# Reordering loads, one weight split and z's transfers in the first phase of a gated-mix kernel

## The chip, the cores and the metric

The kernel runs on one core of a Trainium2 chip. A core has a matrix engine (TensorE, in the profile PE, with its weight loads as PEld), VectorE (DVE), ScalarE (ACT), GpSimd (POOL) and SyncE (SP). Each takes its instructions from a queue of its own, in order. Transfers (DMA) are issued from one of these queues and run beside them on the core's 16 DMA engines. The metric is the device time of one execution in microseconds (us), the median over runs; all times below are us unless marked otherwise.

## The reference

x is 2048 x 512, all in float32. One gate per row mixes two branches.

```python
x = A_x
g = sigmoid((x * gate_w).sum(-1, keepdims=True))
# branch a: linear attention, 32 heads of 16
q, k, v = split_heads(x @ wqkv)
pq, pk = q @ w_phi[h], k @ w_phi[h]                      # per head
phi_q = concat([softmax(pq), softmax(-pq)])              # per head, over 16
phi_k = concat([softmax(pk), softmax(-pk)])
kv = phi_k^T v            ;  z = phi_k summed over all rows
a = (phi_q kv) / (phi_q z + 1e-6) @ wo
# branch b: 512 -> 1376 -> 512
b = mish(x @ w1 + b1) @ w2
out = g * a + (1 - g) * b
```

## The kernel before

**Precision.** Every matmul operand is split into a high part (rounded to fp32r) and a low part (the rest), and each product is three matmuls: high by high, high by low, low by high. So each weight piece and each piece of x needs an ACT step that makes the high part and a DVE or POOL step that subtracts to get the low part.

**Phases.** Phase A walks over x in eight chunks of 256 rows (index 0 to 7; "chunk four" is index 3) and makes q, k, v, the exponentials of k's features, and the sums kv and z. Phase B walks over four blocks of 512 rows: the two big matmuls of branch b (`up`, `down`), phi_q, and the output. While phase A runs, w1, w2 and wo are loaded piece by piece and split, ready for phase B.

**Order.** The order is written out by hand: a text of short names per chunk (FIRST, SECOND, THIRD, FOURTH, SEVEN for index 4 and 5, NEXT for 6, LAST for 7) and per block. `run` (line 209) walks a text and emits the named step; an apostrophe means the step of the chunk before, a plus the first block of phase B, a hash a step of the weights. Each instruction is pinned in that order on its own engine's queue; steps of different engines meet only through their data, their buffers, and the `behind` calls below. In SEVEN the words `more`, `rest` and `late` are replaced by lists of weight steps that differ between index 4 and 5 (lines 886 to 890).

**The steps that the change and the prediction touch**, with the engine of each:

- `ldx` (SP, line 156): loads x two chunks ahead, 512 KB, into one of two buffers of the tag "tx". The sums that `sa` makes stand in buffers of the same tag. `xh` (ACT) and `xl` (DVE, line 258) split the next chunk's x; `sa` (POOL, line 339) forms four sums and differences of it, which `sh0 sh1` (ACT) and `sl0 sl1` (POOL, line 349) split. Index 2 to 5 use these in a scheme with fewer products (matmul steps `s1` to `s7`).
- `mx mn d0 d1` (DVE): per head maximum and minimum of k's features, and the differences, into a tile E; `E` (ACT): its exponential; `S rS` (DVE): sums and reciprocals; `ml` (DVE, line 297): scales E by them. The number behind is the half of the chunk (0 or 1).
- `kk` (PE): the matmuls into `kvp` for two chunks, from E and v. `v0 v1` and `ve0 ve1` make v (PE, ACT); `qe st` copy q (ACT) and store it (SP).
- `z` : up to index 4 a transfer, issued by POOL, that adds E to a sum in DRAM (line 454). `zld` (SP, line 462) loads one such sum into `zacc`, `za` (POOL, line 465) adds the other by a transfer; from index 5 on `z` is a POOL addition to `zacc` (line 452).
- `Lj Hj Oj`: load (SP, line 169), high part (ACT) and low part (POOL, line 526) of weight piece j. Pieces 0 to 2 are w1a, 3 to 5 w1b, 6 to 8 w2a, 9 to 11 w2b. The loads go into two buffers of the tag "oh" in turn, so a load waits for the `O` of the piece two before it in the order of loading (0 1 2 3 4 5 11 7 8 9 6 10).
- `behind(...)` (line 293): makes a POOL step wait for the last DVE step named in `dve[0]` at that place of the text; `ml`, `xl` and phase B's `d1` set it. `O`, `sl1` and the additions of `z` carry it.
- In NEXT, `ldx`, `ldw0`: x for phase B's first block; `ldw1`: half of wo; `lq0+`: q of the first block. `up` of phase B takes `xbh` and then `xbl` (line 559), which are x's halves for the block.

Of the kernel before, what the change touches and what calls it, by code (L numbers as in the profile page):

```python
# [41 lines left out]
    S0 rS0 ml0 S1 rS1 ml1 q0 qe0 st0 q1 qe1 st1  # L42
"""
SECOND = """
    h0# h1# sa z0' z1' k0 mx0 mn0 d00 d10 k1 E0 L0# L1# xh mx1 mn1 d01 d11 v0 E1 S0 rS0 ve0 sh0 ml0 xl sl0 z0 ldx
    v1 S1 rS1 ml1 ve1 q0 qe0 st0 q1 qe1 st1 t2# sh1
"""
THIRD = """
# [1 line left out]
    S0 s5 qa rS0 s4 st1 mx1 mn1 d01 d11 s3 qe0 st0 ml0 O1# L3# z0  # L50
"""
FOURTH = """
    s1 bc E1' S1' rS1' ml1' ve1' s7 m7 sh1' s2 xh s6 ca xl sl1' sa z1' H2# O2# L4# mx0 mn0 d00 d10 E0 ldx v0 ve0 sh0 sl0 H3#
    s4 s5 qa st1 S0 rS0 mx1 mn1 d01 d11 v1 s3 qe0 st0 ml0 O3# L5# z0
"""
SEVEN = """
    s1 bc E1' S1' rS1' ml1' ve1' s7 m7 sh1' s2 kk xh xl sl1' zld sa z1' more mx0 s6 ca mn0 d00 d10 E0 ldx v0 ve0 sh0 sl0 za rest S0 rS0
    s4 s5 qa st1 mx1 mn1 d01 d11 E1 ml0 late v1 S1 rS1 s3 ve1 qe0 st0 ml1
"""
NEXT = """  # L60
    lq0+ k0 xh xl mx0 mn0 k1 kk d00 d10 ldx H9# E0 O9# ldw0 L10# z0' z1' mx1 mn1 d01 d11 H6# E1 S0 rS0 ml0 O6# ldw1 v0 ve0
    S1 rS1 ml1 v1 ve1 q0 mx0+ mn0+ d00+ d10+ z0 z1 qe0 st0 q1 qe1 st1 H10# O10# E0+ lq1+
"""
LAST = """
    k0 mx0 mn0 d00 d10 k1 E0 XH0 kv' mx1 mn1 d01 d11 E1 v0 S0 rS0 ml0 z0 ve0 ldo XH1 mx1+ mn1+ S1 rS1 ml1 d01+ d11+
# [33 lines left out]
def tile_gated_mix(ctx: ExitStack, tc: tile.TileContext, xT, wv, wkT, wqT, bd, w1a, w1b, b1, w2a, w2b, wo, out):  # L99
# [109 lines left out]
    def run(text, key, prev=None, nxt=None):  # L209
        for w in text.split():  # L210
            k = prev if w.endswith("'") else nxt if w.endswith("+") else "W" if w.endswith("#") else key
            for fn in steps.pop((k, w.rstrip("'+#")), ()):
                fn()
# [670 lines left out]
    run(THIRD, ("A", 2), ("A", 1))  # L884
    run(FOURTH, ("A", 3), ("A", 2))
    for c in FAST[2:]:
        w = {4: ("", "H4# O4# L11# H5#", "O5# L7# z0"), 5: ("H11# O11# L8# H7# O7# L9#", "", "H8# O8# L6#")}[c]
        text = SEVEN
        for name, part in zip(("more", "rest", "late"), w):
            text = text.replace(name, part)  # L890
        run(text, ("A", c), ("A", c - 1))
    for c, text in ((NCH - 2, NEXT), (NCH - 1, LAST)):
# [64 lines left out]
```

## Time and profile before

| what | us |
|---|---|
| median of 3 runs | 449.32 (448.28 to 449.78) |
| the profiled execution: its time | 449.89 |
| its span, first to last instruction | 448.2 |
| PE busy in the span | 439.8 |
| DVE, ACT, POOL busy | 322.2, 210.7, 158.7 |
| phase A, until the first `up` that reads `xbl` | 151.6 |

How to read it: a busy PE is a PE with a matmul in its pipeline; the matmuls' ends are modelled. Rows of the timeline give start, duration, engine, line, operation, the tile written, an arrow and the tiles read, the number of instructions merged, and in brackets the idle time before and what ended it. ACT steps all carry the line of the helper that issues them (131), matmuls line 111; they are told apart by their tiles. The chain of waits is followed back from the last instruction. The queue of SP holds only transfers, so a transfer that waits for its buffer holds back those behind it.

### The profile page before, as it was taken

Reading aid. Unit: us, or ns where it says so; the run is one execution under the profiler, and the core shown is the slowest. Engines: PE = TensorE matmul, PEld = TensorE weight load, DVE = VectorE, ACT = ScalarE, POOL = GpSimd, SP = SyncE. Lnnn points to the kernel's source line nnn. Section 1 sums busy time; section 2 is a strip of 40 time slices with the busy share of each in tenths; the row PEclk is TensorE's granted clock in tenths of the full one; section 3 lists DMA queues with packets and bytes.
Section 4 is the critical chain, followed back from the end, with each engine's and each line's share of the span. In section 5 each row is a group of like instructions: output and inputs, shape, how many; then the busy total and the mean of one; then the engine's idle time right before and its main releaser. Section 6 shows DMA issues by size and latency. Waiting matters only on the chain.

```text
span 448.2 us, 7019 instructions
## 1 busy us (share of the span) xinstructions
PE 439.8 (98%) x2748; PEld 358.8 (80%) x2748; DVE 322.2 (72%) x427; ACT 210.7 (47%) x292; POOL 158.7 (35%) x120
## 2 busy tenths in 40 slices
PE   7999999899999999999999999999999999999996
PEld 6888888788888788788787887887887888787885
DVE  2499789988899999899899967486967529701002
ACT  4774644464455656527275343634253544233220
POOL 2297477675467364312022221113212122221211
PEclk8999999999999999999999999999999999999999
DMA  8424827979934200404352141321141302030002
GB/s 283 165 68 170 187 77 169 236 165 255 312 95 130 93 24 8 122 20 125 114 152 75 47 141 48 94 95 47 42 148 48 88 7 94 2 88 7 0 0 94
DMA packets 27320, 46.35 MB, mean 103 GB/s; under 512 B 5908, under 2 KB 14100, under 8 KB 27288
## 3 DMA queue, kind: packets, MB, share of 16 engines
q1 hardware_dynamic: 25528, 39.88, 29.2%
q0 software_dynamic: 1616, 5.77, 6.7%
q8 instruction: 21, 0.34, 0.3%
q10 hardware_dynamic: 144, 0.26, 0.3%
q14 instruction: 11, 0.09, 0.1%
HBM read 23.87 MB, written 13.64 MB: 84 GB/s over the span
## 4 chain that ended last, share of the span: by engine, by line
PE 65%; DVE 6%; issue 1%
PE up L111 27%; PE down L111 26%; PE wo L111 10%; PE num L111 2%; DVE E L297 1%; DVE Sm L281 1%; DVE E L273 1%; DVE mx L266 1%; DVE E L275 1%; DVE xbl L559 1%; DVE Sm L289 1%; DVE io L797 0%; DVE mn L266 0%; PE z L111 0%; PE kvT L616 0%
## 5 line engine op out<-in xcount | busy, mean ns | idle before, releaser
L662 POOL TENSOR_TENSOR l<-act,h 128x512 fp32r<-128x512 f32 x44 | 61.1, 1390 | 219.0 <-ACT h L131 183.0
L131 ACT ACTIVATE act<-up,b1s 128x512 f32<-128x512 f32 x44 | 30.3, 689 | 86.5 <-PE up L111 86.3
L131 ACT ACTIVATE E<-E 128x1024 f32<-128x1024 f32 x32 | 33.7, 1060 | 52.4 <-DVE E L275 38.9
L297 DVE TENSOR_TENSOR E<-E,Sm 128x1024 f32<-128x1024 f32 x32 | 46.4, 1451 | 1.0
L281 DVE TENSOR_REDUCE Sm<-E 128x64 f32<-128x1024 f32 x32 | 38.7, 1210 | 4.3 <-ACT E L131 4.2
L111 PE MATMUL wo<-woh,ohl 128*128 128x512 f32 x128 | 40.7, 389 | 0.0
L111 PE MATMUL down<-w2ah,h 128*128 128x512 f32 x96 | 37.5, 390 | 0.0
L111 PE MATMUL down<-w2ah,l 128*128 128x512 f32 x96 | 37.4, 389 | 0.0
L111 PE MATMUL down<-w2al,h 128*128 128x512 f32 x96 | 37.3, 389 | 0.0
L797 DVE SCALAR_TENSOR_TENSOR io<-down,og_sb,io 128x512 f32<-128x512 f32 x16 | 11.1, 749 | 31.0 <-PE down L111 31.0
L111 PE MATMUL down<-w2bh,h 128*128 128x512 f32 x80 | 31.2, 390 | 0.0
L111 PE MATMUL down<-w2bl,h 128*128 128x512 f32 x80 | 31.1, 389 | 0.0
L111 PE MATMUL down<-w2bh,l 128*128 128x512 f32 x80 | 31.1, 389 | 0.0
L131 ACT ACT_TABLE_LOAD x20 | 25.7, 1283 | 9.8 <-PE up L111 9.5
L771 DVE TENSOR_TENSOR ohl<-num,ohl 128x512 fp32r<-128x512 f32 x16 | 10.2, 678 | 26.4 <-ACT ohl L131 26.4
L131 ACT ACTIVATE h<-act 128x512 fp32r<-128x512 f32 x44 | 27.8, 632 | 1.4
L111 PEld LDWEIGHTS wo<-woh,ohl 128*128 128x128 f32 x128 | 24.0, 188 | 5.1
L111 PE MATMUL up<-xbh,w1ah 128*128 128x512 f32 x96 | 26.2, 394 | 0.0
L111 PE MATMUL up<-xbl,w1ah 128*128 128x512 f32 x96 | 25.8, 390 | 0.3 <-DVE xbl L559 0.3
L111 PE MATMUL up<-xbh,w1al 128*128 128x512 f32 x96 | 25.7, 389 | 0.0
L559 DVE TENSOR_TENSOR xbl<-xraw,xbh 128x1024 fp32r<-128x1024 f32 x8 | 10.1, 1291 | 21.0 <-ACT xbh L131 21.0
L111 PE MATMUL wo<-wol,ohl 128*128 128x512 f32 x64 | 24.9, 389 | 0.0
(155 smaller groups left out, 1012.4 us busy)
## 6 DMA issues: line engine op xcount, KB each, us to landing
xraw<-in_xT_dram SPq DMA_DIRECT2D x16, 512.0 KB, 5.4
eT<-tt SPq DMA_DIRECT2D x128, 64.0 KB, 2.0
zd<-E POOLq DMA_DIRECT2D x10, 512.0 KB, 6.9
pqd<-qs SPq DMA_DIRECT2D x16, 256.0 KB, 4.5
pq<-pqd SPq DMA_DIRECT2D x16, 256.0 KB, 2.9
out_dram<-io SPq DMA_DIRECT2D x16, 256.0 KB, 2.1
raw<-in_w1a_dram SPq DMA_DIRECT2D x3, 512.0 KB, 4.5
raw<-in_w2a_dram SPq DMA_DIRECT2D x3, 512.0 KB, 5.7
```

Source lines behind the costliest of these rows:

```text
L111: return pin(nc.tensor.matmul(*a, **k))
L131: return pin(A_.activation(out_, in_, fn, **k))
L266: pin(V.tensor_reduce(d[name], hv(src()), axis=AX.X, op=op))
L273: pin(V.tensor_sub(E, hv(src()), d["mx"][:, :, None].to_broadcast([P, H, DH])))
L275: ins = pin(V.tensor_sub(E, d["mn"][:, :, None].to_broadcast([P, H, DH]), hv(src())))
L281: pin(V.tensor_reduce(d["S"], hv(d["E"][:, :]), axis=AX.X, op=ALU.add))
L289: at(key, "rS" + n, lambda: pin(V.reciprocal(d["S"], d["S"])))
L297: dve[0] = pin(eng.tensor_mul(hv(d["E"][:, :]), hv(d["E"][:, :]), d["S"][:, :, None].to_broadcast([P, 2 * H, DH])))
L559: dve[0] = pin(V.tensor_sub(xb[b][1][:, :, sl], kt(raw[h], SC), f32(xb[b][0][:, :, sl])))
L662: pin(G_.tensor_sub(U[i]["l"], U[i]["a"], f32(U[i]["h"])))
L771: pin(V.tensor_sub(ohl[h, gp][:, 512:], num[h, gp], f32(ohl[h, gp][:, :512])))
L797: pin(V.scalar_tensor_tensor(io[t], dn[t], og_sb[:, i : i + 1], io[t], op0=ALU.mult, op1=ALU.add))
```

## The change

Six places of the order texts change; no step is added or taken out.

- SECOND: `L0 L1` go to the head of the text and `ldx` directly behind `sa`.
- FOURTH (index 3): `z1'` goes ahead of `sl1' sa`; `ldx` goes ahead of `H2 O2 L4`; `O3 L5` leave this chunk.
- SEVEN: a new word `early` stands behind `z1'`, which itself moves ahead of `sl1'`. For index 4 it is `O3 L5 sl1'`; for index 5 it is `sl1' ldx`, so the load of chunk index 7 goes ahead of `zld`, `L8` and `L9`. (The `ldx` that stays further on in the text finds its step already emitted at index 5.)
- Index 5's last list: `O8 L6` leave it.
- NEXT: `O8 L6` stand behind `xl`; `z1'` goes behind `ml0`; `O6 ldw1` go behind `ml1`.

```diff
 SECOND = """
-    h0# h1# sa z0' z1' k0 mx0 mn0 d00 d10 k1 E0 L0# L1# xh mx1 mn1 d01 d11 v0 E1 S0 rS0 ve0 sh0 ml0 xl sl0 z0 ldx
+    L0# L1# h0# h1# sa ldx z0' z1' k0 mx0 mn0 d00 d10 k1 E0 xh mx1 mn1 d01 d11 v0 E1 S0 rS0 ve0 sh0 ml0 xl sl0 z0
     v1 S1 rS1 ml1 ve1 q0 qe0 st0 q1 qe1 st1 t2# sh1
 """
 FOURTH = """
-    s1 bc E1' S1' rS1' ml1' ve1' s7 m7 sh1' s2 xh s6 ca xl sl1' sa z1' H2# O2# L4# mx0 mn0 d00 d10 E0 ldx v0 ve0 sh0 sl0 H3#
-    s4 s5 qa st1 S0 rS0 mx1 mn1 d01 d11 v1 s3 qe0 st0 ml0 O3# L5# z0
+    s1 bc E1' S1' rS1' ml1' ve1' s7 m7 sh1' s2 xh s6 ca xl z1' sl1' sa ldx H2# O2# L4# mx0 mn0 d00 d10 E0 v0 ve0 sh0 sl0 H3#
+    s4 s5 qa st1 S0 rS0 mx1 mn1 d01 d11 v1 s3 qe0 st0 ml0 z0
 """
 SEVEN = """
-    s1 bc E1' S1' rS1' ml1' ve1' s7 m7 sh1' s2 kk xh xl sl1' zld sa z1' more mx0 s6 ca mn0 d00 d10 E0 ldx v0 ve0 sh0 sl0 za rest S0 rS0
+    s1 bc E1' S1' rS1' ml1' ve1' s7 m7 sh1' s2 kk xh xl z1' early zld sa more mx0 s6 ca mn0 d00 d10 E0 ldx v0 ve0 sh0 sl0 za rest S0 rS0
     s4 s5 qa st1 mx1 mn1 d01 d11 E1 ml0 late v1 S1 rS1 s3 ve1 qe0 st0 ml1
 """
 NEXT = """
-    lq0+ k0 xh xl mx0 mn0 k1 kk d00 d10 ldx H9# E0 O9# ldw0 L10# z0' z1' mx1 mn1 d01 d11 H6# E1 S0 rS0 ml0 O6# ldw1 v0 ve0
-    S1 rS1 ml1 v1 ve1 q0 mx0+ mn0+ d00+ d10+ z0 z1 qe0 st0 q1 qe1 st1 H10# O10# E0+ lq1+
+    lq0+ k0 xh xl O8# L6# mx0 mn0 k1 kk d00 d10 ldx H9# E0 O9# ldw0 L10# z0' mx1 mn1 d01 d11 H6# E1 S0 rS0 ml0 z1' v0 ve0
+    S1 rS1 ml1 O6# ldw1 v1 ve1 q0 mx0+ mn0+ d00+ d10+ z0 z1 qe0 st0 q1 qe1 st1 H10# O10# E0+ lq1+
 """
@@
-        w = {4: ("", "H4# O4# L11# H5#", "O5# L7# z0"), 5: ("H11# O11# L8# H7# O7# L9#", "", "H8# O8# L6#")}[c]
+        w = {
+            4: ("O3# L5# sl1'", "", "H4# O4# L11# H5#", "O5# L7# z0"),
+            5: ("sl1' ldx", "H11# O11# L8# H7# O7# L9#", "", "H8#"),
+        }[c]
         text = SEVEN
-        for name, part in zip(("more", "rest", "late"), w):
+        for name, part in zip(("early", "more", "rest", "late"), w):
             text = text.replace(name, part)
         run(text, ("A", c), ("A", c - 1))
```

More of the change, by code (lines that the diff above doesn't have):

```diff
@@ L44 @@
 SECOND = """
-    h0# h1# sa z0' z1' k0 mx0 mn0 d00 d10 k1 E0 L0# L1# xh mx1 mn1 d01 d11 v0 E1 S0 rS0 ve0 sh0 ml0 xl sl0 z0 ldx
+    L0# L1# h0# h1# sa ldx z0' z1' k0 mx0 mn0 d00 d10 k1 E0 xh mx1 mn1 d01 d11 v0 E1 S0 rS0 ve0 sh0 ml0 xl sl0 z0
     v1 S1 rS1 ml1 ve1 q0 qe0 st0 q1 qe1 st1 t2# sh1
@@ L52 @@
 FOURTH = """
-    s1 bc E1' S1' rS1' ml1' ve1' s7 m7 sh1' s2 xh s6 ca xl sl1' sa z1' H2# O2# L4# mx0 mn0 d00 d10 E0 ldx v0 ve0 sh0 sl0 H3#
-    s4 s5 qa st1 S0 rS0 mx1 mn1 d01 d11 v1 s3 qe0 st0 ml0 O3# L5# z0
+    s1 bc E1' S1' rS1' ml1' ve1' s7 m7 sh1' s2 xh s6 ca xl z1' sl1' sa ldx H2# O2# L4# mx0 mn0 d00 d10 E0 v0 ve0 sh0 sl0 H3#
+    s4 s5 qa st1 S0 rS0 mx1 mn1 d01 d11 v1 s3 qe0 st0 ml0 z0
 """
 SEVEN = """
-    s1 bc E1' S1' rS1' ml1' ve1' s7 m7 sh1' s2 kk xh xl sl1' zld sa z1' more mx0 s6 ca mn0 d00 d10 E0 ldx v0 ve0 sh0 sl0 za rest S0 rS0
+    s1 bc E1' S1' rS1' ml1' ve1' s7 m7 sh1' s2 kk xh xl z1' early zld sa more mx0 s6 ca mn0 d00 d10 E0 ldx v0 ve0 sh0 sl0 za rest S0 rS0
     s4 s5 qa st1 mx1 mn1 d01 d11 E1 ml0 late v1 S1 rS1 s3 ve1 qe0 st0 ml1
@@ L60 @@
 NEXT = """
-    lq0+ k0 xh xl mx0 mn0 k1 kk d00 d10 ldx H9# E0 O9# ldw0 L10# z0' z1' mx1 mn1 d01 d11 H6# E1 S0 rS0 ml0 O6# ldw1 v0 ve0
-    S1 rS1 ml1 v1 ve1 q0 mx0+ mn0+ d00+ d10+ z0 z1 qe0 st0 q1 qe1 st1 H10# O10# E0+ lq1+
+    lq0+ k0 xh xl O8# L6# mx0 mn0 k1 kk d00 d10 ldx H9# E0 O9# ldw0 L10# z0' mx1 mn1 d01 d11 H6# E1 S0 rS0 ml0 z1' v0 ve0
+    S1 rS1 ml1 O6# ldw1 v1 ve1 q0 mx0+ mn0+ d00+ d10+ z0 z1 qe0 st0 q1 qe1 st1 H10# O10# E0+ lq1+
 """
```

## The prediction

> **What bounds the kernel now.** I read the page first, then the waits of TensorE (PE), then the chain that ended last. The page gives the size of the prize, and a mean DMA rate for each slice of 11.2 us (the tenth, 100.8 to 112.0 us: 255 GB/s).
>
> ```profile
> span 448.2 us, 7019 instructions
> PE 439.8 (98%) x2748; PEld 358.8 (80%) x2748; DVE 322.2 (72%) x427; ACT 210.7 (47%) x292; POOL 158.7 (35%) x120
> ...
> GB/s 283 165 68 170 187 77 169 236 165 255 312 95 130 93 24 8 122 20 125 114 152 75 47 141 48 94 95 47 42 148 48 88 7 94 2 88 7 0 0 94
> ```
>
> PE waits for whom (total, times, longest); two other rows, left out, belong to the first microseconds, far ahead of the edited chunks:
>
> ```profile
> PE kvp L111 <- DVE E L297: 1.2, 1, 1.2
> ...
> PE up L111 <- DVE xbl L559: 0.3, 1, 0.3
> ```
>
> So a reordering in the chunks can win at most the waits at `kvp` (`kk`, in chunk index 4) and at `up` (the first matmul of phase B that reads `xbl`). The chain shows how the second comes about: VectorE (DVE) is the last link until 151.56, PE from there to the end.
>
> ```profile
> 149.28 2.28 DVE xbl L559 x2
> ...
> 151.60 3.92 PE up L111 x16
> ```
>
> Everything after 151.6 is PE work that the diff doesn't touch, so the time moves by what PE reaches `up`'s third part earlier or later. PE's rows at the first wait (start, duration; in brackets the idle time before it and its releaser):
>
> ```profile
> 82.68 1.55 PE L111 MATMUL kvp<-E,v 128*32 128x64 f32 x96
> 85.39 0.65 PE L111 MATMUL kvp<-E,v 128*32 128x64 f32 x32 [1.17 <-DVE E L297]
> ```
>
> **What sets those two waits.** DVE's timeline around both places: E<-E,Sm is the scaling `ml`, Sm<-E the sum `S1` of chunk index 3, xl<-xraw,xh the low half of chunk index 7.
>
> ```profile
> 79.39 2.25 DVE L297 TENSOR_TENSOR E<-E,Sm 128x1024 f32<-128x1024 f32 x1
> 81.69 1.22 DVE L281 TENSOR_REDUCE Sm<-E 128x64 f32<-128x1024 f32 x1
> ...
> 83.53 1.72 DVE L297 TENSOR_TENSOR E<-E,Sm 128x1024 f32<-128x1024 f32 x1
> ...
> 96.35 1.22 DVE L297 TENSOR_TENSOR E<-E,Sm 128x1024 f32<-128x1024 f32 x1
> ...
> 114.94 3.04 DVE L297 TENSOR_TENSOR E<-E,Sm 128x1024 f32<-128x1024 f32 x1
> 119.46 1.29 DVE L258 TENSOR_TENSOR xl<-xraw,xh 128x512 fp32r<-128x512 f32 x2 [1.48 <-ACT xh L131]
> ...
> 127.28 2.04 DVE L297 TENSOR_TENSOR E<-E,Sm 128x1024 f32<-128x1024 f32 x1
> ...
> 131.07 1.97 DVE L297 TENSOR_TENSOR E<-E,Sm 128x1024 f32<-128x1024 f32 x1
> ```
>
> GpSimd's (POOL) timeline beside it:
>
> ```profile
> 76.61 2.69 POOL L526 TENSOR_TENSOR w1al<-raw,w1ah 128x1024 fp32r<-128x1024 f32 x1
> 78.97 1.59 POOL L349 TENSOR_TENSOR w2bl<-sraw,w2bh 128x512 fp32r<-128x512 f32 x1
> 81.77 2.40 POOL L526 TENSOR_TENSOR w1bl<-raw,w1bh 128x1024 fp32r<-128x1024 f32 x1 [1.22 <-ACT E L131]
> ...
> 93.88 2.49 POOL L526 TENSOR_TENSOR w1bl<-raw,w1bh 128x1024 fp32r<-128x1024 f32 x1
> ...
> 104.38 0.89 POOL L454 DMA_DIRECT2D zd<-E  x1
> ...
> 114.50 2.39 POOL L526 TENSOR_TENSOR w2al<-raw,w2ah 128x1024 fp32r<-128x1024 f32 x1 [2.03 <-ACT w2ah L131]
> ...
> 123.33 4.90 POOL L452 TENSOR_TENSOR zacc<-zacc,E 128x1024 f32<-128x1024 f32 x2
> 129.55 2.40 POOL L526 TENSOR_TENSOR w2al<-raw,w2ah 128x1024 fp32r<-128x1024 f32 x1 [1.32 <-DVE E L297]
> ```
>
> Laid side by side: alone, `ml` takes 1.22. Each longer one ends about 1.1 after the POOL row that ran when it started: 114.50+2.39 is 116.89, and the `ml` of 114.94 ends at 117.98; 81.77+2.40 is 84.17, and the `ml` of 83.53 ends at 85.25. So a scaling waits out the running POOL tensor operation, and an `O` step placed beside it costs DVE up to 1.8.
>
> ScalarE (ACT): xh<-xraw are the high halves of x, w2ah<-raw the steps `H8` and `H6`, E<-E the exponentials `E1`.
>
> ```profile
> 80.60 1.05 ACT L131 ACTIVATE E<-E 128x1024 f32<-128x1024 f32 x1
> ...
> 85.44 1.15 ACT L131 ACTIVATE xh<-xraw 128x512 fp32r<-128x512 f32 x2 [2.30 <-DMA xraw<-in_xT_dram]
> ...
> 113.35 1.06 ACT L131 ACTIVATE w2ah<-raw 128x1024 fp32r<-128x1024 f32 x1 [0.28 <-DMA raw<-in_w2a_dram]
> ...
> 114.79 0.59 ACT L131 ACTIVATE qs<-proj 128x512 f32<-128x512 f32 x1
> 118.79 1.15 ACT L131 ACTIVATE xh<-xraw 128x512 fp32r<-128x512 f32 x2 [3.41 <-DMA xraw<-in_xT_dram]
> ...
> 124.19 1.05 ACT L131 ACTIVATE w2ah<-raw 128x1024 fp32r<-128x1024 f32 x1
> 125.61 1.06 ACT L131 ACTIVATE E<-E 128x1024 f32<-128x1024 f32 x1 [0.38 <-PE proj L111]
> ```
>
> SyncE's (SP) issues, and from issue to landing the x loads (first of the two rows) and the weight pieces of line 169 (second):
>
> ```profile
> 79.77 0.43 SPq L156 DMA_DIRECT2D xraw<-in_xT_dram  x1
> ...
> 91.90 0.33 SPq L156 DMA_DIRECT2D xraw<-in_xT_dram  x1
> ...
> 106.65 0.33 SPq L462 DMA_DIRECT2D zacc<-zd  x1
> 107.08 0.45 SPq L169 DMA_DIRECT2D raw<-in_w2a_dram  x1
> ...
> 109.39 0.38 SPq L156 DMA_DIRECT2D xraw<-in_xT_dram  x1
> ...
> 116.92 0.33 SPq L169 DMA_DIRECT2D raw<-in_w2a_dram  x1
> ```
>
> ```profile
> DMA to landing us min/median/max: 4.1/6.1/9.4
> ```
>
> ```profile
> DMA to landing us min/median/max: 3.0/4.2/5.7
> ```
>
> **The change part by part.** No instruction is added or removed; every term is a wait.
>
> SECOND. SP's sequence there is `L0 L1 ldx st0 st1` with either text, and those of ACT, DVE and POOL don't change. Its load still needs the x buffer that `xl` frees. Cost 0.
>
> FOURTH, `ldx` ahead of `L4`. `L4` needs the buffer of `O2` (POOL, until 79.30), and the load of chunk index 5 stands behind it until 79.77. Its own buffer is free when `sa` ends, which POOL runs before `O2`, so by 76.6: the load leaves at least 3.2 earlier and lands by 82.2 with today's flight; ACT wanted it at 83.1. ACT's 2.30 goes; `L4` leaves with `O2`'s end as now.
>
> FOURTH, `z1'` ahead of `sl1' sa`. The transfer is issued as soon as its E is scaled; `sl1'` waits for `xl` anyway, so POOL loses nothing. `O2` starts some 0.6 earlier, `sl0` with it, and the scaling of 79.39 ends near 80.9 instead of 81.64. That wins nothing by itself: `S1` needs the exponential that ends at 81.65, and started at 81.69.
>
> `O3` a chunk later. The POOL row of 81.77 goes away from the scaling of 83.53: 1.72 becomes 1.22, and **PE's wait at `kvp` falls by 0.50**, from 1.17 to 0.67. What is late next is that same exponential. `O3` now waits for `xl` of chunk index 5 (84.75 + 1.29) and runs from 86.0 to 88.4. `sl1'` follows it until 89.7; PE reads that in `s5`, some 28 matmuls after `kvp`, 0.23 to 0.25 each, near 92: covered by 2, and beyond that PE would stall. `sa` and the load of 91.90 come later by `O3`'s 2.40 less what `xl` gains (the 0.5 and about 0.9 of ACT's wait): near 1. That load has no wait in ACT's rows today; if it lands just in time now, it costs ACT up to 1 in chunk index 5, otherwise 0, which I take. `L5` leaves at 88.4 instead of 84.2, lands at the longest (5.7) by 94.1, and is wanted by `O5`, behind `O4` (until 96.37): covered. DVE, ahead by up to 1 in this chunk, loses it again to `O4`: the scaling of 96.35 cannot end before 96.37+1.1, and ends at 97.57 now.
>
> Chunk index 5, `z1'` ahead of `sl1'`: issued some 3.5 before 104.38; again POOL waits for `xl` behind it. `ldx` ahead of `zld L8 L9`: `zld` waits for a z transfer until 106.65, and the x load behind all three leaves at 109.39. Now it leaves when `sl1'` has freed a buffer, by 104.4 (the z row of 104.38 follows `sl1'` today), and lands by 113.8 even at 9.4. Then `xh` of chunk index 7 is bound by ACT's own order, `H8 ve1 qe0`, done at 115.38 today. `zld L8 L9` wait for later things than the x load, so they leave as now or within a microsecond, 107.1 to 108.
>
> `O8` and `L6` into NEXT. `O8` leaves the scaling of 114.94: 3.04 becomes 1.22, 1.8 of DVE. It now runs behind `xl`; `L6`, which needs its buffer, leaves after that. `H6` and the exponential `E1` of chunk index 6 stand behind `L6` on ACT: this is what is late next. `z1'` put behind `ml0`, and `O6` behind `ml1`, leave the scaling of 131.07 alone (0.75); that of 127.28 meets `z0'` as before.
>
> The end of phase A, with t for the landing of `L8` (113.35 now). `xh` starts at t+2.0 (113.35 to 115.38), `xl` ends at t+4.0 (the 1.96 from 118.79 to 120.75), `O8` at t+6.4 (2.40), `L6` lands at t+12.1 (5.7), `H6` and `E1` end at t+14.2 (1.05 + 1.06), the sum and its reciprocal take 1.84 (81.69 to 83.53), `ml1` 1.22: t+17.3. Today `ml1` ends at 133.04. The unknown is t: flights of 3.0 to 9.4 from 107.1 to 108 give 110.1 to 117.4. I take the flight that this very load has now, 6.3, and 113.8. Then `ml1` ends at 131.1, 1.9 earlier, and from there to `xbl` DVE's work is the same. PE comes to `up` 0.50 earlier and finds `xbl` ready: **the wait of 0.3 goes too**. Sum: -0.50 - 0.30 = -0.8. The profiled execution took 449.89 (span 448.2), so 449.1 there; the median of the runs, 449.32, lies 0.57 below it: 448.5.
>
> **A rule that speaks against it.** The row of 107.08 is `L8`, today issued ahead of the x load of 109.39. The Trainium skill, DMA: Bandwidth & Descriptors, section "Queues, rings and completion order", says that on each DMA engine the descriptors of one ring are consumed in ring order; by that `L8` would pay for the load put ahead of it, and the sum would be -0.3 rather than -0.8. No row before shows two SP loads exchanged.
>
> **The rivals.** (1) The x load is paid for by the weights: its 512 KB at 255 GB/s are 2.06 ahead of `L8`, t = 115.4, `ml1` at 132.7, DVE only 0.3 ahead. PE arrives 0.5 earlier and waits for it: -0.3, 449.0. For it: the x load took 9.4 in this spell. Against: it leaves 3 to 5 before `L8`, so most of a flight of 4.1 to 6.1 is over by then. (2) Slower: `L8` takes 9.4, as the x load does now, from 108: t = 117.4, `ml1` at 134.7, and PE waits at `up` 1.7 longer than the chain shows: 451.0. It decides from t = 115.7, where `ml1` is at 133.04 again. For it: `H8` sits ahead of `xh` on ACT, and the new chain hangs on two landings, the old on one. Against: 9.4 is the longest of all rows, and `L8`'s own is 6.3. (3) The whole wait at `kvp` goes, 1.17 + 0.3: 447.85. It would need `S1` to start 0.7 before the exponential of 80.60 has ended; nothing in the diff moves that.
>
> **How the numbers follow.** Forecast 0.48, (1) 0.17, (2) 0.21, (3) 0.14, the last also for what a spread of 1.5 over three runs can do. 0.3% is 1.35 us, about what a measurement of this kernel can tell from no change. Forecast and (1) lie within it: 0.65 same; (3) is just over it: 0.14 faster; (2): 0.21 slower. The range goes from (3), a little lower, to (2): 447.7 to 451.0. The likeliest case's own is 448.2 to 449.0.
>
> **What would show it.** Right: `kvp` waits about 0.7 and `up` not at all; `xh` of chunk index 7 starts near 115.8 without a wait for its load; no scaling from 83 to 135 over 1.3 but the two beside `O4` and `z0'`; `E1` of chunk index 6 starts near 127, behind `H6`. Wrong: ACT waits of more than 2 for w2a pieces near 113 or 125, an `up` wait over 0.3, or a new PE wait between 86 and 150.

## The result, and the profile after

| what | before | after |
|---|---|---|
| median of 22 runs each | 449.54 (448.28 to 450.61) | 448.61 (447.63 to 449.99) |
| the profiled execution: its time | 449.89 | 448.44 |
| its span | 448.2 | 446.7 |

The ratio of after to before is 0.9979, with a 95% interval from 0.9969 to 0.9989: 0.9 us faster (0.5 to 1.4 by the interval), a gain clear of the noise, though within the 0.3% that the prediction counts as the same. The forecast was 448.5.

First, the span and the engines' busy time from the page of after, then PE's waits (total, times, longest):

```profile
span 446.7 us, 7023 instructions
PE 438.3 (98%) x2748; PEld 357.3 (80%) x2748; DVE 319.6 (72%) x427; ACT 210.9 (47%) x292; POOL 158.6 (36%) x120
```

```profile
PE fuse L111 <- DMA wT<-in_wkT_dram: 2.5, 2, 1.8
...
PE kvp L111 <- DVE E L297: 0.7, 1, 0.7
```

The wait at `kvp` has shrunk from 1.2 to 0.7 and that at `up` is gone. The first row, at the very start, belongs to loads that nothing edited; it differs from execution to execution. PE's timeline of after at the two marks that matter, the first `kvp` of all and the one of the prediction:

```profile
48.27 1.99 PE L111 MATMUL kvp<-E,v 128*32 128x64 f32 x128
...
55.02 0.50 PE L111 MATMUL proj<-w2ah,w2bh 128*128 128x512 f32 x1 [0.23 <-issue]
...
82.22 1.55 PE L111 MATMUL kvp<-E,v 128*32 128x64 f32 x96
84.45 0.65 PE L111 MATMUL kvp<-E,v 128*32 128x64 f32 x32 [0.69 <-DVE E L297]
```

The first `kvp` stands at 49.23 in the profile before and at 48.27 here; over all profiles of this study it stands between 48.16 and 50.15, whichever text the kernel has up to there. So of the 1.5 between the two spans, 1.0 is a start that happened to be quicker, and a better reading of one profile is from the first `kvp` to the end of the span: 399.0 before (448.2 - 49.23), 398.4 after (446.7 - 48.27). The table of experiments below gives this figure too.

That figure still holds an accident. From the first `kvp` to the second, PE took 33.95 in after, and 33.42 to 33.47 in every other profile, also in that of o8_back, whose text is the same up to there: the 0.5 were lost around the row of 55.02, of which 0.23 show as idle time. From the second `kvp` to the first `up` that reads `xbl` it took 68.92 before (82.68 to 151.60) and 67.90 after (82.22 to 150.12): there the change is worth 1.0 in this pair of profiles.

The chain of waits of after, from start to end of the stretch around `kvp` and then around `up` (start, duration, what):

```profile
80.16 1.06 ACT E L131
...
81.24 1.23 DVE Sm L281
...
83.08 1.24 DVE E L297
...
84.45 0.65 PE kvp L111 x32
...
147.21 1.03 PE kvp L111 x64
148.25 5.66 PE up L111 x24
```

What is late now at `kvp` is the exponential, then the sum, then the scaling, one directly behind the other. At `up` there is no DVE link any more. DVE's timeline of after shows why (rows as in the prediction; E<-pq,mx is the subtraction `d0` of phase B's first block):

```profile
78.95 1.38 DVE L297 TENSOR_TENSOR E<-E,Sm 128x1024 f32<-128x1024 f32 x1
81.24 1.22 DVE L281 TENSOR_REDUCE Sm<-E 128x64 f32<-128x1024 f32 x1 [0.92 <-ACT E L131]
83.08 1.23 DVE L297 TENSOR_TENSOR E<-E,Sm 128x1024 f32<-128x1024 f32 x1
...
95.30 1.80 DVE L297 TENSOR_TENSOR E<-E,Sm 128x1024 f32<-128x1024 f32 x1
...
113.90 1.22 DVE L297 TENSOR_TENSOR E<-E,Sm 128x1024 f32<-128x1024 f32 x1
...
117.54 0.68 DVE L273 TENSOR_TENSOR E<-proj,mx 128x512 f32<-128x512 f32 x1
...
122.96 1.75 DVE L297 TENSOR_TENSOR E<-E,Sm 128x1024 f32<-128x1024 f32 x1
...
127.29 1.23 DVE L297 TENSOR_TENSOR E<-E,Sm 128x1024 f32<-128x1024 f32 x1
129.62 2.08 DVE L273 TENSOR_TENSOR E<-pq,mx 128x512 f32<-128x512 f32 x1
...
146.07 2.35 DVE L559 TENSOR_TENSOR xbl<-xraw,xbh 128x1024 fp32r<-128x1024 f32 x2
```

The scalings that took 1.72, 3.04 and 1.97 take 1.23, 1.22 and 1.23. `ml1` of chunk index 6 ends at 128.52 (127.29 + 1.23) instead of 133.04, and `xbl` starts at 146.07 instead of 149.19. ACT and SP of after, around chunk index 5:

```profile
102.90 1.06 ACT L131 ACTIVATE w2ah<-raw 128x1024 fp32r<-128x1024 f32 x1 [1.25 <-DMA raw<-in_w2a_dram]
...
112.55 1.06 ACT L131 ACTIVATE w2ah<-raw 128x1024 fp32r<-128x1024 f32 x1 [0.53 <-DMA raw<-in_w2a_dram]
114.47 1.16 ACT L131 ACTIVATE xh<-xraw 128x512 fp32r<-128x512 f32 x2
...
123.40 1.06 ACT L131 ACTIVATE w2ah<-raw 128x1024 fp32r<-128x1024 f32 x1 [3.44 <-DMA raw<-in_w2a_dram]
124.37 1.04 ACT L131 ACTIVATE E<-E 128x1024 f32<-128x1024 f32 x1
```

```profile
98.55 0.33 SPq L169 DMA_DIRECT2D raw<-in_w2a_dram  x1
...
101.96 0.33 SPq L156 DMA_DIRECT2D xraw<-in_xT_dram  x1
...
106.61 0.38 SPq L169 DMA_DIRECT2D raw<-in_w2a_dram  x1
...
118.93 0.33 SPq L169 DMA_DIRECT2D raw<-in_w2a_dram  x1
```

The three rows of the w2a pieces are `H7`, `H8`, `H6`, and their loads `L7`, `L8`, `L6`. `xh` of chunk index 7 no longer waits for its load. `L8` leaves at 106.61 and `H8` starts, having waited for it, at 112.55: t of the prediction is 112.55, a flight of 5.9.

### The profile page after: what moved, and what is told of

Read it like the earlier page. It is cut to its first block, busy times and chain, and to the rows that moved or that the text cites. A ratio compares the mean times of both kernels' runs of the same rounds, so it can differ in the third digit from the quotient of the medians.

```text
span 446.7 us, 7023 instructions
## 1 busy us (share of the span) xinstructions
PE 438.3 (98%) x2748; PEld 357.3 (80%) x2748; DVE 319.6 (72%) x427; ACT 210.9 (47%) x292; POOL 158.6 (36%) x120
## 4 chain that ended last, share of the span: by engine, by line
PE 96%; DMA 1%; DVE 1%; issue 0%; SPq 0%; ACT 0%; ACTq 0%
PE proj L111 28%; PE up L111 27%; PE down L111 27%; PE wo L111 10%; PE num L111 2%; PE kvp L111 1%; DMA wT<-in_wkT_dram 1%; PE fuse L111 1%; DVE io L797 0%; DVE E L297 0%; DVE Sm L281 0%; ACT E L131 0%; PE z L111 0%; SPq L159 0%; DVE Sm L289 0%
## 5 line engine op out<-in xcount | busy, mean ns | idle before, releaser
L662 POOL TENSOR_TENSOR l<-act,h 128x512 fp32r<-128x512 f32 x44 | 60.1, 1367 | 220.7 <-ACT h L131 184.7
L297 DVE TENSOR_TENSOR E<-E,Sm 128x1024 f32<-128x1024 f32 x32 | 42.3, 1321 | 1.0
```

Of the source, the lines that this page charges most:

```text
L297: dve[0] = pin(eng.tensor_mul(hv(d["E"][:, :]), hv(d["E"][:, :]), d["S"][:, :, None].to_broadcast([P, 2 * H, DH])))
L662: pin(G_.tensor_sub(U[i]["l"], U[i]["a"], f32(U[i]["h"])))
```

## The experiments

Each ratio is to the kernel before, run beside it on the same chip, with its 95% interval; the kernel before had medians of 449.63 to 449.81 there, and the ratio isn't simply that of the medians (z_back's would be 1.0009). The last column is the span less the start of the first `kvp`, from the one profiled execution of each. That execution isn't always a typical one: in x_back and e1_alone it is the slowest of the twelve, in o3_only the second fastest.

| kernel | median | ratio | from the first `kvp` on |
|---|---|---|---|
| before | 449.54 | | 399.0 |
| after | 448.61 | 0.9979 [0.9969, 0.9989] | 398.4 |
| head_only | 448.38 | 0.9973 [0.9960, 0.9986] | 397.9 |
| tail_only | 449.56 | 0.9993 [0.9977, 1.0009] | 399.0 |
| o3_only | 453.42 | 1.0064 [1.0042, 1.0086] | 399.1 |
| o3_again (o3_only, one execution) | 452.08 | | 401.3 |
| o3_x5 | 450.49 | 1.0020 [0.9999, 1.0041] | 397.8 |
| x7_only | 449.08 | 0.9994 [0.9979, 1.0008] | 398.4 |
| x_back | 449.27 | 0.9991 [0.9977, 1.0005] | 399.4 |
| z_back | 450.09 | 0.9995 [0.9978, 1.0012] | 400.1 |
| o8_back | 448.61 | 0.9976 [0.9964, 0.9988] | 397.9 |
| e1_alone | 449.52 | 0.9997 [0.9979, 1.0015] | 399.9 |
| e1_first | 448.13 | 0.9961 [0.9947, 0.9974] | 397.9 |
| head_e1 | 448.00 | 0.9956 [0.9940, 0.9973] | 397.6 |

The theory at the start: the gain is the prediction's two terms, the `kvp` term from `O3` alone, and the `up` term from DVE's lead, which the edits of index 5 and NEXT make. Against it: that the x loads carry the gain, or z's transfers, which the prediction gave no worth.

### o3_only: the weight split alone, a chunk later

```diff
 FOURTH: ... qe0 st0 ml0 O3# L5# z0   ->  ... qe0 st0 ml0 z0
 index 4: kk xh xl sl1' zld sa        ->  kk xh xl O3# L5# sl1' zld sa
```

> The kernel before with one edit alone: O3 and L5 a chunk later (behind xl in chunk index 4). Theory (two waits, one behind the other): the scaling ml1 of chunk index 3 takes 1.2 instead of 1.7, PE's kvp wait falls from 1.2 to about 0.7, but DVE's end of phase A does not come earlier, so the wait at up grows from 0.3 to about 0.8 and the time stays: -0.1 to +0.2 us, ratio 1.000. Rival (the kvp wait is worth its 0.5 on its own, DVE follows): up wait stays at 0.3, time -0.5 us, ratio 0.999.

The `kvp` wait fell to 0.7 as said, and the kernel became 0.6% slower: the theory that this move is neutral or better by itself fell. Its twelve executions lie in two groups, three at 449.7 to 450.3 and nine at 452.5 to 454.5, and the profiled one, 450.06, was of the first. It has no wait at `up` either, where the theory had 0.8, but PE had lost 0.92 before that in a gap without a releaser. The next profile is one of the longer group.

### o3_again: where the two microseconds are

> The kernel o3_only once more, for another profile: most of its executions took 452.5 to 454.5 us, its profiled one 450.1. Theory (O3 behind a late xl pushes POOL's sl1', sa and O4 back, and PE waits for sl1 in s5 or for a later step): an execution near 453 shows a proj wait of 2 to 4 us on PE between 88 and 105. Rival (PE's own instruction stream comes late through the busy DMA engines; o3_only's profile has a wait of 0.9 for nothing that is shown, in the middle of v0): the wait of 3 us has no releaser and falls inside a group of matmuls.

At 452.08 this execution is close to the longer group. The chain on POOL is that of the theory, but PE's wait stands later than 88 to 105, and it has a releaser, against the rival. PE's, ACT's, POOL's and SP's timelines of o3_again:

```profile
113.31 0.73 PE L111 MATMUL proj<-wqh,w2bh 128*128 128x512 f32 x2 [2.08 <-DVE qs L430]
```

```profile
108.86 1.06 ACT L131 ACTIVATE w2ah<-raw 128x1024 fp32r<-128x1024 f32 x1 [5.56 <-DMA raw<-in_w2a_dram]
109.83 1.04 ACT L131 ACTIVATE E<-E 128x1024 f32<-128x1024 f32 x1
```

```profile
87.79 2.38 POOL L526 TENSOR_TENSOR w1bl<-raw,w1bh 128x1024 fp32r<-128x1024 f32 x1 [5.10 <-DVE xl L258]
```

```profile
101.51 0.33 SPq L169 DMA_DIRECT2D raw<-in_w2a_dram  x1
```

Read from the end: PE waits 2.08 for `qa` (written qs, line 430), a DVE step of chunk index 5. That stands behind the sum of `E0`, and `E0` stands behind `H7` on ACT. `H7` waits 5.56 for `L7`. `L7` leaves at 101.51, where it left at 99.02 before, since the splits whose buffer it needs are late; and it then flies 7.3 instead of 4.4. Leaving late isn't enough for that: in o3_only's profile `L7` leaves as late, at 101.62, but flies 4.5, and PE doesn't wait there. `O3` is the first of those late splits: it waits 5.10 for an `xl` that is itself late, because the x load of index 5 still stands behind `L4`.

### o3_x5: the same, with the x load of chunk index 5 ahead

```diff
 on top of o3_only
 FOURTH: sl1' sa z1' H2# O2# L4# mx0 ... E0 ldx v0  ->  sl1' sa z1' ldx H2# O2# L4# mx0 ... E0 v0
```

> o3_only with the x load of chunk index 5 ahead of L4 besides; z1' stays where it was. Theory (the pieces hang together: O3 in its new place is cheap only if xl, which it waits for, is early): xl of chunk index 5 ends 1.5 to 2 us earlier than in o3_only, O3 and what follows it on POOL with it, and the time falls back to that of before, 449.3 to 450.0, kvp wait 0.7, up wait 0.3 to 0.8. Rival (moving O3 costs by itself): 453 again.

Most of the loss comes back: 1.0020 against 1.0064. Its profiled execution is a good one (`L7` at 99.58, `H7` at 104.04, no PE wait but 0.7 at `kvp`), yet the median, 450.49, is above the 449.3 to 450.0 of the theory and no better than before. So the x load is one part of what `O3` needs, not all of it. The next kernel, head_only, shows the other part: it differs from o3_x5 in the places of `z1'` in index 3 and 4 alone, ran on the same chip, and its median is 2.1 lower (448.38), with intervals that lie apart (0.9960 to 0.9986, and 0.9999 to 1.0041).

### head_only: the edits of index 3 and 4 alone

```diff
 FOURTH as in the change
 index 4: z1' O3# L5# sl1' sa          (index 5 and NEXT as before: sl1' zld sa z1', O8# L6# late)
```

> The kernel before with only the edits of FOURTH and of chunk index 4 (z1' ahead, ldx ahead of L4, O3 L5 later); chunk index 5 and NEXT as before. Theory (the gain at kvp is handed back at up unless DVE's end comes earlier too): kvp wait 0.7, up wait 0.6 to 1.0, time that of before, -0.2 to +0.2 us. Rival (each half is worth its own wait): -0.5 us, ratio 0.999, up wait 0.3.

The whole gain is here, 0.9973. The `up` wait is gone as well, which my theory gave to the edits of index 5 and NEXT: that part fell. DVE's, POOL's and ACT's rows in chunk index 5:

```profile
114.04 1.22 DVE L297 TENSOR_TENSOR E<-E,Sm 128x1024 f32<-128x1024 f32 x1
116.94 1.73 DVE L258 TENSOR_TENSOR xl<-xraw,xh 128x512 fp32r<-128x512 f32 x2 [1.68 <-ACT xh L131]
```

```profile
114.61 2.91 POOL L526 TENSOR_TENSOR w2al<-raw,w2ah 128x1024 fp32r<-128x1024 f32 x1 [0.98 <-ACT w2ah L131]
```

```profile
116.28 1.15 ACT L131 ACTIVATE xh<-xraw 128x512 fp32r<-128x512 f32 x2 [0.78 <-DMA xraw<-in_xT_dram]
```

`O8` is still beside the scaling here, but it came second, and it is `O8` that takes longer. The Trainium skill, SBUF — State Buffer, section "Who interferes with whom", has it that a DVE operation with both inputs in SBUF contends with GpSimd's reads and that the order of issue decides who blocks. The rows agree: before, `O8` came first (114.50) and the scaling took 3.04; here the scaling came first and took 1.22, while `O8` took 2.91 instead of 2.39.

But the short scaling is not what took the `up` wait away: behind it DVE waits 1.68 for `xh` of chunk index 7, as it waited 1.48 before, and o8_back below has no wait at `up` with a scaling of 3.40 in this place. What came earlier is `xh`, which waits for its x load: it starts 67.38 after the first `kvp`, where it started 69.56 after it before. The load left at 108.49 and flew 7.8; before it left at 109.39 and flew 9.4. Why it flew shorter isn't shown.

### tail_only: the edits of index 5 and NEXT alone

```diff
 index 5: z1' sl1' ldx zld sa, late: H8#     (FOURTH and index 4 as before)
 NEXT as in the change
```

> The kernel before with only the edits of chunk index 5 and of NEXT (z1' and ldx ahead, O8 L6 behind xl, z1' behind ml0, O6 behind ml1); FOURTH and chunk index 4 as before. Theory: the kvp wait stays 1.2, the up wait goes, as DVE ends phase A 2 to 3 us earlier: time -0.3 to -0.45 us, ratio 0.999. Rival (the two halves depend on each other, the tail wins only where PE already comes earlier): no change, up wait 0.3.

No gain that can be told from none: 0.9993, the interval on both sides of 1; the theory's 0.999 lies in it too. The profile has the waits of the theory: `xbl` starts at 146.15 and PE doesn't wait for it, but PE still waits 1.2 at `kvp`. A wait of 0.3 for the high half `xbh` stands at 223.41, in the next block of phase B.

### x7_only: the x load of chunk index 7 alone

```diff
 index 5: sl1' zld sa ...  ->  sl1' ldx zld sa ...
```

> The kernel before with the x load of chunk index 7 ahead of zld, L8 and L9, nothing else. Theory (there is room in the spell from 102 to 107): L8 lands as now, H8's wait stays under 0.8, xh of chunk index 7 starts at 115.4 to 116.5 instead of 118.8; but O8 still holds the scaling ml1 until 118, so xl ends near 119.3, 1.4 earlier, and the up wait goes: -0.3 to -0.45 us. Rival (ring order: L8 pays for the load ahead of it): H8 waits 2 us more, xh starts near 117.5 or later, the same or slower than before.

0.9994, again with an interval on both sides of 1. The profile has no wait at `up`, though the scaling beside `O8` takes 3.06: the x load alone takes that wait away. This is also the direct measure of the prediction's first rival, in ACT's row of `H8`:

```profile
112.74 1.06 ACT L131 ACTIVATE w2ah<-raw 128x1024 fp32r<-128x1024 f32 x1 [0.31 <-DMA raw<-in_w2a_dram]
```

`L8` leaves at 106.90, so its flight is 5.8; it was 6.3 with nothing put ahead of it. The x load ahead of it doesn't lengthen it.

### x_back: the change with both x loads at their old places

```diff
 FOURTH: sa ldx H2# O2# L4# ... E0 v0  ->  sa H2# O2# L4# ... E0 ldx v0
 index 5: sl1' ldx                     ->  sl1'
```

> The kernel after with the x loads of chunk index 5 and 7 put back to their old places (behind E0), all else kept. Theory (the x loads are worth DVE time, not PE time, as long as DVE's lead lasts): ACT waits for xraw again, 2 us near 85 and 2 to 4 us near 118; xl of chunk index 7 ends 2 to 4 us later than with the change and L6 with it; DVE's lead at xbl falls from about 3 us to 0 to 1; kvp wait stays 0.7; time between that of the change and +0.5 over it. Rival (the loads carry the gain): up wait comes back with 0.8 or more and the time is that of before.

0.9991: nearer to 1 than to the 0.9979 of the change, but the interval holds both. PE's timeline near the end of phase A, in the slowest of the twelve executions:

```profile
149.52 0.65 PE L111 MATMUL kvp<-E,v 128*32 128x64 f32 x32 [0.36 <-DVE E L297]
...
152.90 1.20 PE L111 MATMUL up<-xbl,w1ah 128*128 128x512 f32 x4 [0.69 <-DVE xbl L559]
```

In this execution DVE's lead is gone without the early x loads, and the wait at `up` is larger than in the profile before the change. Of the two loads head_only has that of chunk index 5 early and that of index 7 in its old place, and it has the whole gain: that points to the load of index 5 as the one needed.

### z_back: the change with z's transfers at their old places

```diff
 FOURTH: xl z1' sl1' sa ldx            ->  xl sl1' sa z1' ldx
 SEVEN:  xh xl z1' early zld sa more   ->  xh xl early zld sa z1' more
 NEXT:   z0' mx1 ... ml0 z1' v0        ->  z0' z1' mx1 ... ml0 v0
```

> The kernel after with all z1' back in their old places (behind sa in FOURTH and chunk index 4, behind the loads in index 5, ahead of ml0 in NEXT). Theory (a z transfer's issue costs POOL 0.9 and only pushes what POOL does next): in FOURTH O2 and sl0 end 0.6 to 0.7 later, ml0 of chunk index 3 ends near 81.6 again, but S1 waits for the exponential anyway; kvp wait 0.7, no up wait, time that of the change within 0.2 us. Rival (the z transfers carry part of the gain): kvp wait over 0.9, or 0.4 us and more slower than the change.

I gave these moves no worth, and that fell: 0.9995, nine of its twelve executions at 449.7 or more, where the kernel before has a median of 449.68 beside it and o8_back one of 448.61. ACT, SP and PE of z_back:

```profile
106.60 1.06 ACT L131 ACTIVATE w2ah<-raw 128x1024 fp32r<-128x1024 f32 x1 [5.47 <-DMA raw<-in_w2a_dram]
```

```profile
98.79 0.33 SPq L169 DMA_DIRECT2D raw<-in_w2a_dram  x1
```

```profile
111.05 0.74 PE L111 MATMUL proj<-wqh,w2bh 128*128 128x512 f32 x2 [1.75 <-DVE qs L430]
```

It is the place of o3_again: `H7` late, `E0` behind it, PE waiting for `qa`. Here `L7` leaves as early as in after (98.79 against 98.55), but flies 7.8 instead of 4.35. The places of `z1'` in index 3 and 4, two of those put back here, are the ones that part o3_x5 from head_only.

### o8_back: the change with O8 and L6 at their old places

```diff
 index 5, late: H8#          ->  H8# O8# L6#
 NEXT: xh xl O8# L6# mx0     ->  xh xl mx0
```

> The kernel after with O8 and L6 back in chunk index 5's last list. Theory (O8 stands in ml1's way and costs 1.8 of DVE, which the lead of 3 at xbl covers; L6 in return leaves 2 earlier): ml1 of chunk index 5 takes 2.5 to 3.0, the second exponential of chunk index 6 no longer waits for H6, DVE's lead falls by 0 to 1.5, no up wait, time that of the change. Rival (O8's place is what removed the up wait): up wait 0.3 or more, 0.3 to 0.5 us slower than the change.

0.9976: nothing is lost. The scaling beside `O8` takes its long time again, and PE has no wait behind that at `kvp`:

```profile
113.74 3.40 DVE L297 TENSOR_TENSOR E<-E,Sm 128x1024 f32<-128x1024 f32 x1
```

So DVE's 2.2 in that place are not what the gain hangs on, once the x loads and `O3` have given DVE its lead.

### e1_first, e1_alone, head_e1: the exponential ahead of `bc`

```diff
 SEVEN: s1 bc E1' S1' rS1' ml1'  ->  s1 E1' bc S1' rS1' ml1'
 e1_first: on top of the change;  e1_alone: on top of before;  head_e1: on top of head_only
```

> The kernel after with one more edit: in SEVEN the exponential E1' of the chunk before goes ahead of s1 and bc, so ACT runs it ahead of the copy bc. Theory (what is late at kvp is the exponential behind bc): E1' starts 0.6 to 1.1 earlier, S1, rS1 and ml1 with it, the kvp wait of 0.7 goes to 0 to 0.1, and PE is gapless from 17 us to the end: 0.6 us below the change, ratio 0.9965 to before. Rival (bc, now later by 0.4 to 0.5, holds back s6 and ca, and PE waits there): a proj wait of 0.3 to 0.6 near 85 takes its place, time that of the change.

> The kernel before with one edit alone: in SEVEN the exponential E1' goes ahead of the copy bc (as in e1_first, without the change). Theory (two causes stand one behind the other at kvp: POOL's operations beside the scalings, then the exponential): ml0 still ends at 81.6, so S1 starts at 81.7 as before, ml1 still waits for O3, kvp waits 1.1 to 1.2 and the time is that of before, ratio 0.9995 to 1.0005. Rival (the exponential alone was the cause): kvp wait 0.5 to 0.7, -0.5 us.

> head_only (FOURTH and chunk index 4 of the change) with E1' ahead of bc. Theory (all that pays is in chunk index 3 and 4, and PE has no other wait in phase A): kvp wait 0, up wait 0, 0.6 to 0.7 below head_only: 447.7 to 448.0, ratio 0.996, as e1_first. Rival (with PE 0.7 earlier DVE's lead without the tail's edits is used up): up wait of 0.2 or more, time that of head_only.

This tests what is left of the `kvp` wait. In e1_first, ACT's exponential and PE's `kvp`:

```profile
79.27 1.06 ACT L131 ACTIVATE E<-E 128x1024 f32<-128x1024 f32 x1 [0.17 <-DVE E L273]
```

```profile
82.45 1.99 PE L111 MATMUL kvp<-E,v 128*32 128x64 f32 x128
```

The exponential starts 3.18 ahead of the `kvp` matmuls, where it starts 2.06 ahead of them in after (80.16 to 82.22), and they run as one block of 128 without a wait. PE is not quite gapless behind that: 0.20 without a releaser at 86.68, 0.15 for `xbh` at 223.09. In e1_alone the exponential is early too, but the two scalings still stand beside POOL's splits, and the wait stays at 1.16:

```profile
79.84 2.26 DVE L297 TENSOR_TENSOR E<-E,Sm 128x1024 f32<-128x1024 f32 x1
...
83.85 1.86 DVE L297 TENSOR_TENSOR E<-E,Sm 128x1024 f32<-128x1024 f32 x1
```

So the wait had two causes, one behind the other: first the scalings beside POOL, then the exponential. Moving the exponential alone shows nothing; taking the split away alone shows 0.5 of 1.2. head_e1, which is the edits of index 3 and 4 and this one, has the lowest median of all, 448.00 and 0.9956, from seven executions; its interval overlaps those of e1_first and of head_only. So the wait is shown to go, but what that is worth in time, some 0.2% by the medians, can't be told from no difference by these intervals.

## Why the prediction came out right, point by point

**The `kvp` term, -0.50:** 1.17 became 0.69, so -0.48, by the mechanism named: `O3` is away and the scaling takes 1.23. The exponential is next, as said; e1_first shows that this is all that is left.

**The `up` term, -0.30:** the wait is gone, and it was worth more than the idle time in its brackets. PE's rows before, then after:

```profile
150.26 1.07 PE L111 MATMUL up<-xbh,w1al 128*128 128x512 f32 x4
151.60 1.20 PE L111 MATMUL up<-xbl,w1ah 128*128 128x512 f32 x4 [0.27 <-DVE xbl L559]
```

```profile
149.21 1.07 PE L111 MATMUL up<-xbh,w1al 128*128 128x512 f32 x4
150.12 1.07 PE L111 MATMUL up<-xbl,w1ah 128*128 128x512 f32 x4
```

From one group of matmuls to the next it was 1.34 and is 0.91: 0.43 less. Without a wait the rows overlap by 0.16, which the idle time leaves out. `ml1` of chunk index 6 was put at 131.1 and ends at 128.5. Half of these 2.6 is t, 112.55 instead of 113.8, most of it the quicker start; the other half lies behind t, 16.0 to the end of `ml1` instead of 17.3, since `L6` flew 4.5 (118.93 to 123.40) where the sum had the longest of its view, 5.7. `E1` of index 6 stands behind `H6`, which waits 3.44 for `L6`, as said. The prediction also has an ACT wait of more than 2 for a w2a piece near 125 among its signs of being wrong. This sign came and PE lost nothing by it: the chain that it added up has ACT waiting for `L6` itself, so the sign was badly chosen.

**The sum:** -0.8 forecast, -0.9 between the medians, and 0.48 + 0.43 = 0.91 in the two profiles. The two terms fit that; how closely is in part luck, as each kernel spreads over 2 us and the interval of the gain goes from 0.5 to 1.4. There is luck of another kind in it too: the sum would have been the same for z_back, where no gain can be told from none, so it held because the change moves `z1'` along with the rest.

**The covers:** `L5`, `sl1'` and the x load of 91.90 (92.42 now) cost PE nothing; DVE lost its lead to `O4` as said, in the scaling of 95.30 (1.80). SECOND's edit is in neither head_only nor head_e1, which have the gain.

**Rival (1), that `L8` pays for the x load:** it didn't, with 5.9 in after and 5.8 in x7_only against 6.3. The x load took 8.2 from 101.96, so it landed by 110.2, before `L8`'s end at 112.55. The ring order of the Trainium skill, DMA: Bandwidth & Descriptors, section "Queues, rings and completion order", is not contradicted by that: the load ahead did land first, it only cost `L8` nothing that shows. The price of this rival was worked out from today's 113.35; from the forecast's own 113.8 its t would be 115.9, past the 115.7 at which nothing is left of the `up` term. **Rival (2)** needed `L8` to take 9.4. **Rival (3)** needed the exponential moved, which e1_first and head_e1 did, to 0.9961 and 0.9956.

Steps that failed, though the sum held:

- **"z1' ahead of sl1' sa ... POOL loses nothing", "that wins nothing by itself".** POOL lost nothing, but z_back loses the gain, and the same `z1'` moves in index 3 and 4 make 2.1 between o3_x5 and head_only. The prediction priced POOL and DVE and looked at `L8` and `L6`; it had no line for `L7`, `H7` and the `E0` of chunk index 5 behind it. That `E0` waits 1.53 for DVE before, behind `H7`, so `L7` has some 1.5 of slack; a flight of 7.3 or 7.8 instead of 4.4 overruns it, and PE waits 2.08 or 1.75.
- **`O3` as a step with a worth of its own.** By itself it is 0.6% slower. It is cheap only with the x load of index 5 early and `z1'` ahead of it (head_only); with the x load alone it isn't fully (o3_x5).
- **The lead of DVE at `up`, given to index 5 and NEXT.** They do bring it (tail_only, and x7_only with the x load alone), but head_only gets it without these edits, and o8_back without the moves of `O8` and `L6`.
- **"`O6` behind `ml1`" taken as free.** There it meets phase B's `d0`: 128.74 to 131.14 on POOL, and the `d0` of 129.62 takes 2.08 instead of 0.68. That gives back 1.4 of DVE's lead, hidden here.

**Left open.** Why `L7` flies 4.2 to 4.5 in eleven of the profiles, 6.2 in one (x7_only) and 7.3 to 7.8 in two: o3_only (4.5) and o3_again (7.3) are the same kernel. z's transfers go out on POOL beside it. In the eight profiles with `z1'` of index 4 in its old place three flights are over 6 (x7_only, o3_again, z_back); in the six with it ahead none is. That fits the gain of these moves, but three of eight against none of six doesn't show that they cause it. Nor is it shown that the nine longer executions of z_back, or the spread in o3_x5, are all of this kind.

## What to carry to other kernels

For each piece of work that is moved, list every load and split that stands in an in-order queue ahead of a critical step, with its slack, also where the move doesn't touch it: here the one without a line in the sum (`L7`, `H7`, `E0`) held PE back in the profiles of o3_again and z_back. Undo the parts of a change one by one before any of them is called free or good, since here one part alone cost 0.6% and was worth its gain only with two others, the x load of index 5 and the `z1'` moves, one of which had been priced at nothing. Where a wait remains smaller than it was, look for the second cause behind the first: with the exponential ahead of `bc` the rest of the wait at `kvp` went too.

## What the runs showed of the hardware that was not expected

- A 512 KB load from one place of one kernel took 4.5 us in one execution and 7.3 in another (`L7` in o3_only and o3_again); in the second PE waited 2.08 for what stood behind it.
- Of two DVE subtractions beside a POOL split the one with both inputs in SBUF was slowed. In after, the `d0` of 117.54 reads the matmul's result in PSUM and takes 0.68 beside the `O8` of 116.52; the `d0` of 129.62 reads two tiles in SBUF and takes 2.08 beside `O6`; that of 144.86, with POOL idle, takes 0.69:

```profile
116.52 2.38 POOL L526 TENSOR_TENSOR w2al<-raw,w2ah 128x1024 fp32r<-128x1024 f32 x1 [3.84 <-DVE xl L258]
...
128.74 2.40 POOL L526 TENSOR_TENSOR w2al<-raw,w2ah 128x1024 fp32r<-128x1024 f32 x1 [1.48 <-DVE E L297]
```

- PE sat idle for 0.2 to 0.9 us in the middle of groups of matmuls without any wait that the profile shows (0.23 at 55.02 in after, 0.90 in e1_alone, 0.92 in o3_only). No run was made on that.
